# Row stores of the tail bunched behind the last attention values, and slot 1's row gathers moved behind the last store

## The chip, the cores and the metric

One NeuronCore of a Trainium2 chip runs the whole program. The metric is the device time in microseconds (us) of one execution. TensorE is called PE, VectorE DVE, ScalarE ACT, GpSimd POOL and SyncE SP; "PE issue" in the profile is time in which PE waited for nothing that the profile shows.

## The reference

Chunked attention feeds a mixture of experts with one expert per row. The attention works on 8 x 8 heads of 576 rows in chunks of 64; its output, 4608 rows of 512, is routed.

```python
scores = scale * np.matmul(q_c, k_c.transpose(0, 1, 2, 4, 3))
attn = np.exp(scores - max); attn = attn / (sum + 1e-09)
x = np.matmul(attn, v_c) ...            # (4608, 512)
logits = x @ w_gate                      # 8 experts
expert_idx = np.argmax(logits, axis=1)
gate_w = softmax(logits)[row, expert_idx]
out[mask] = gate_w * (np.maximum(x[mask] @ w1[e], 0.0) @ w2[e])   # for each expert e
```

## The kernel before

**Attention stage.** The 4608 rows are 36 tiles of 128 rows, in 18 groups of two tiles (the loop over `g`). Per group PE computes scores, transposes and values (`attn_v`, L283: 64 small matmuls into the banks U and V); DVE scales the values into a row buffer `xb` (`x_out`, L295); PE transposes the rows once more (`x_t`, L306) and makes the logits (`logits`, L318, then `sel_`, L899). Seven batches of tiles (6, 6, 6, 6, 4, 4, 4) go through `route`, a generator whose small DVE steps are dealt out between other work by `small_op` and `side_op`. It ends with a row index `di` (L401) for each row of the batch; POOL writes gate and row number into the buffer (L403); and the batch's tiles enter the list `waiting`.

**Sorting by expert.** `store(n, after)` (L417 to L428) takes the first `n` waiting tiles and has POOL scatter each one's 128 rows to the DRAM array `xd`, sorted by expert, with an indirect DMA (L424). Where `after` is given, ACT first copies one column of that tile into the unused last column of the first of these tiles (L422), so that the first store waits for it; this is how the kernel sets the pace of the stores. `gather(u)` (L548) fetches the two blocks of 128 rows of slot `u` from `xd` into `xg`, `gather_x(u)` (L552) a third block into `xg3`, each with an indirect DMA on POOL's queue (L543). The first two slots of expert 0 need not wait for all rows: slot 0 takes rows of the first 18 tiles, slot 1 of the first 32. `early(k)` computes their indices and, once those tiles are stored, issues `gather(k)` (L501). A gather reads `xd` as a whole for the scheduler, so it waits for all stores issued before it, and a store issued after it waits for the gather to have read.

**Expert stage.** A slot is 256 rows (and up to 128 more) through one expert: `make_xt` (L566 to L569) transposes the gathered rows and splits them into two parts, `gemm1` (L586, L593 with the extra rows) and `gemm2` (L662 to L664) multiply, `finish` (L671) scales and POOL scatters the output (L672). Slot 0 is cut into 32 half steps, the "halves" of the generator `fill`; `filler(n)` puts n of them on PE between the last steps of the attention, and a 33rd step finishes it.

**The tail.** Behind the loop L979 to L1061 order the rest by hand; all engines run in program order. In order: last transposes, `attn_v` of group 17, and the last logits, routing and index tables, with fillers in between; a loop `while active` that ends with the tables; then `store(NMAX)` (NMAX is 6), `gather_x(1)`, weight loads for slot 2 (`load_w`, L528, 1 MB each), the remaining halves, `make_xt(1)`, and slot 1.

Of the kernel before, what the change touches and what calls it, by code (L numbers as in the profile page):

```python
# [8 lines left out]
F32 = mybir.dt.float32  # L9
# [21 lines left out]
NMAX = max(BATCHES)  # L31
# [14 lines left out]
def attn_moe_kernel(ctx: ExitStack, tc: tile.TileContext, q, k, v, wg, w, out):  # L46
# [164 lines left out]
    def quads(i, hp):  # L211
        for c in range(2):
            for m in range(2):
                o = hp * 128 + c * 64
                yield (slice(c * 64, (c + 1) * 64), m, slice((i * 4 + hp) * 64, (i * 4 + hp + 1) * 64),
                       slice(m * 64, (m + 1) * 64), slice(o, o + 64), (m * 64, c * 64))
# [36 lines left out]
    def soft_c(ex):  # L253
        su = sm.tile([P, NH, 1], F32, name="su", bufs=2)
        nc.vector.tensor_reduce(su.rearrange("p (m h) o -> p m (h o)", m=2),
                                ex.rearrange("p h m k -> p m h k"), AX.X, ALU.add)
        return su

    def soft_e(su):
        suf = su.rearrange("p h o -> p (h o)")  # L260
        nc.scalar.activation(suf, suf, AF.Copy, bias=1e-9)
# [7 lines left out]
    def attn_t(ex):  # L269
        at = sp.tile([P, G, 4, 128], F32, name="at", bufs=1)  # L270
        for i in range(G):
            pt = bank("TQ", [P, 4, 128])
            for hp in range(4):
                nc.tensor.transpose(pt[:, hp, :], ex[:, i * 4 + hp, :, :].rearrange("p m k -> p (m k)"), ident)
            nc.scalar.copy(at[:, i, :, :], pt)
        return at

    def attn_v(g, at):
        px = [one["U"], one["V"]]
        for i in range(G):  # L280
            for hp in range(4):
                for po, m, fo, pi, fi, at_ in quads(i, hp):
                    nc.tensor.matmul(px[m][po, fo], at[pi, i, hp, po], vb[g % NB][pi, i, fi],  # L283
                                     start=True, stop=True, tile_position=at_)
        return px
# [131 lines left out]
    def store(n, after=None):  # L417

        for k, (b, i, t, di) in enumerate(waiting[:n]):
            x = xb[t // RB % XB][:, t % RB, :]  # L420
            if k == 0 and after is not None:
                nc.scalar.copy(x[:, XW - 1:XW], after)  # L422
            stored.add(t)
            nc.gpsimd.indirect_dma_start(  # L424
                out=xds[b % 2 * NMAX + i],
                out_offset=bass.IndirectOffsetOnAxis(ap=di[:, i, :], axis=0),
                in_=x, in_offset=None, bounds_check=NT - 1, oob_is_err=False)
        del waiting[:n]  # L428
# [4 lines left out]
    def advance(kind, side=False):  # L433


        for x in active:
            if x[1] == kind and x[2] == side and not (kind == "t" and r_live[0]):
                x[1] = next(x[0], "end")
                if x[1] == "end":
                    active.remove(x)  # L440
                return
# [28 lines left out]
    def early(k):  # L470


        B = EARLY[k]
        c0_ = sm.tile([P, B], F32, name=f"c{k}", bufs=1)
        st = sm.tile([P, B], F32, name=f"st{k}", bufs=1)
        ge = sm.tile([P, 2, B], F32, name=f"ge{k}", bufs=1)
        su = sm.tile([P, 2], F32, name=f"su{k}", bufs=1)
        S5 = [P, 2, B]
        n0 = ce[:, 0, 0:B]
        at_ = pid_h[:, 0:2] if k == 0 else g1[:, 0:2]  # L480
        yield "v"
        nc.vector.tensor_tensor_scan(c0_, n0, n0, 0.0, ALU.add, ALU.bypass)
        yield "v"
        nc.vector.memset(st[:, B - 1:B], BIG)
        yield "v"
        nc.vector.tensor_tensor(st[:, 0:B - 1], rows_b[:, 0:B - 1], n0[:, 0:B - 1], ALU.subtract)
        yield "v"
        nc.vector.tensor_tensor(ge, at_.unsqueeze(2).broadcast_to(S5),
                                c0_.unsqueeze(1).broadcast_to(S5), ALU.is_ge)
        yield "v"  # L490
        nc.vector.tensor_copy((msk0, msk1)[k][:, 0:2], ge[:, :, B - 1])
        yield "v"
        nc.vector.tensor_tensor(ge, ge, st.unsqueeze(1).broadcast_to(S5), ALU.mult)
        yield "v"
        nc.vector.tensor_reduce(su, ge, AX.X, ALU.add)
        yield "v"
        nc.vector.tensor_tensor((idx0, idx1)[k][:, 0:2], su, at_, ALU.add)
        yield None
        while not stored.issuperset(range(TE[k])):
            yield None  # L500
        gather(k)  # L501
        yield "v"
        if k == 0:
            nc.vector.tensor_scalar(add[0], c0_[:, B - 1:B], -1.0, float(BLK), ALU.mult, ALU.add)
        else:
            nc.vector.scalar_tensor_tensor(add[1], c0_[:, B - 1:B], -1.0, add[0], ALU.mult, ALU.subtract)
            yield "v"
            nc.vector.tensor_scalar(add[1], add[1], 2.0 * BLK, None, ALU.add)
        yield "v"
        nc.vector.tensor_scalar(add[k], add[k], 0.0, None, ALU.max)  # L510
        yield "v"
        if k == 0:
            nc.vector.tensor_scalar(g1, pid_h, add[0], float(BLK), ALU.subtract, ALU.add)
        else:

            nc.vector.tensor_tensor(add[1], add[1], add[0], ALU.add)
            yield "v"
            nc.vector.tensor_scalar(g1[:, 2:3], pid_h[:, 2:3], add[1], float(BLK),
                                    ALU.subtract, ALU.add)
# [21 lines left out]
    def rows_in(t, u, h):  # L541
        rows = TE[u] * P if u < 2 and h < 2 else NT
        nc.gpsimd.indirect_dma_start(  # L543
            out=t[:, :], out_offset=None, in_=xd[0:rows, :],
            in_offset=bass.IndirectOffsetOnAxis(ap=place(u, h), axis=0),
            bounds_check=rows - 1, oob_is_err=False)

    def gather(u):  # L548
        for h in range(2):
            rows_in(xg[u % 2][h], u, h)  # L550

    def gather_x(u):  # L552
        rows_in(xg3, u, 2)
# [65 lines left out]
    lo_, h0 = [], []  # L619
# [7 lines left out]
    def slot_0():  # L627

        py = None
        for i, step in enumerate(BLOCKS):  # L630
            f = BLOCKS[:i].count(step)
            flush()
            if step == "1":
                ph = bank("S", [P, BLK])
                gemm1_pe(0, f, ph, range(2))
                yield
                gemm1_pe(0, f, ph, range(2, 4))
                lo_.append((ph, relu_hi(ph)))
            else:
                if py is None:  # L640
                    py = [bank(x, [P, D]) for x in "UV"]
                gemm2(0, f, h0[f], 0, py)
                yield
                gemm2(0, f, h0[f], 1, py)
            yield
        for m in range(2):
            finish(0, m, py[m])

    def filler(n):
        for _ in range(n):  # L650
            next(fill, None)
            halves[0] -= 1

    fill, halves = slot_0(), [2 * len(BLOCKS)]
# [234 lines left out]
    st_e, st_l, st_x = {}, {}, {}  # L889
# [21 lines left out]
    def pauses():  # L911
        for x in list(active):
            if x[1] is None:
                x[1] = next(x[0], "end")
                if x[1] == "end":
                    active.remove(x)
# [17 lines left out]
    for g in range(NG):  # L934
# [9 lines left out]
        if ga >= 0:  # L944
            at = attn_t(st_e[ga])
            su = soft_c(st_e.pop(ga))
# [16 lines left out]
        if ga >= 0:  # L963
            px = attn_v(ga, at)
# [14 lines left out]
    g = NG - 1  # L979
# [3 lines left out]
    small_op(5)  # L983
    ex = st_e.pop(g)
    at = attn_t(ex)
    store(2, at[:, 0, 0, 0:1])
    filler(1)
    su = soft_c(ex)
    soft_e(su)
    store(1, su[:, 0, :])  # L990
    advance("a")
    st_x[g - 1] = x_t(g - 1, xb[(g - 1) * G // RB % XB])
    store(2, st_x[g - 1][:, 0, 0:1])
    pauses()
    small_op(7)
    advance("a")
    px = attn_v(g, at)
    filler(2)
    ri = soft_d(su)
    x_out(g, px, ri, xb[g * G // RB % XB])  # L1000
    logits(g - 1)
    store(1, st_l[g - 1][:, 0:1])
    filler(1)
    advance("t")
    small_op(5)
    advance("a")
    filler(1)
    st_x[g] = x_t(g, xb[g * G // RB % XB])
    store(2, st_x[g][:, 0, 0:1])
    sel_(g - 1)  # L1010
    filler(1)
    side_op(4)
    logits(g)
    store(2, st_l[g][:, 0:1])
    assert stored.issuperset(range(TE[1]))
    filler(1)
    sel_(g)
# [13 lines left out]
    while active:  # L1031
        for x in "cat":
            advance(x)
        small_op(2)
        pauses()
        side_op(3)
        if halves[0] > 5:
            filler(1)
        if halves[0] % 2 and h0:
            store(1, h0[-1][0][:, 0:1].bitcast(F32))  # L1040
    store(NMAX)
    assert len(stored) == NTILE
    gather_x(1)
    load_w(2, 0)
    load_w(2, 1)
# [10 lines left out]
    filler(2)  # L1056
    for c in range(2, 4):
        load_w(2, c)
    filler(halves[0] - 4)
    make_xt(1, banks="QK")  # L1060
    filler(5)  # L1061
    def slot(u, kd, nxt):
        par = wset(u)
        py = [bank("UV"[m], [P, D]) for m in range(2)]
# [127 lines left out]
```

## Time and profile before

| | |
|---|---|
| median of 3 runs | 636.71 us (634.97 to 638.28) |
| profiled execution | 635.64 us, of which 633.8 us span |
| PE busy | 588.0 us, 93% of the span |
| DVE, ACT, POOL busy | 409.7, 298.6, 271.1 us |
| mean granted clock of PE | 0.979 |

Times below are us from the start of the span. The granted clock has two levels, 1.00 (2.4 GHz) and 0.50 (1.2 GHz). A row of a timeline gives start, duration, engine, line, operation, output and inputs; in brackets the idle time of the engine before it and what ended it.

### The profile page before, as it was taken

What the parts mean: (1) busy time and instruction counts of PE and PEld (TensorE: products, weight loads), DVE (VectorE), ACT (ScalarE), POOL (GpSimd) and SP (SyncE); (2) the same over time, 40 slices, a digit from 0 to 9 for tenths busy, and PEclk for the clock granted to TensorE, in tenths of its full rate; (3) what the DMA queues carried; (4) which work ended last, traced back from release to release, by engine and by line L of the source; (5) the groups of instructions that cost most, each with busy time, mean ns of one, the idle gap of its engine ahead of it and who ended that gap; (6) DMA issues with size and microseconds to landing.
All of it is one profiled execution on the core that took longest, in us unless ns stands there. A gap on an engine that the chain in (4) does not pass through costs nothing. (4 is left out here: it accounts for less than half of the span.)

```text
span 633.8 us, 14583 instructions
## 1 busy us (share of the span) xinstructions
PE 588.0 (93%) x5775; PEld 515.8 (81%) x5775; DVE 409.7 (65%) x814; ACT 298.6 (47%) x561; POOL 271.1 (43%) x277
## 2 busy tenths in 40 slices
PE   7796979879989999999899999999899999999994
PEld 5575867758779989988798879999799899899893
DVE  6687789964836667666375647666546676676663
ACT  2565556642223455554255435544434455555452
POOL 2123445463434256435163226535412564464372
PEclk9999799997979999999999999999999999999998
DMA  8989799532284262156025402247520226421011
GB/s 315 394 279 346 244 336 314 193 140 96 100 314 156 78 198 82 36 170 218 5 72 194 157 6 77 69 163 263 205 68 29 67 72 228 124 73 36 2 35 35
DMA packets 31902, 94.88 MB, mean 150 GB/s; under 512 B 11488, under 2 KB 11488, under 8 KB 28192
## 3 DMA queue, kind: packets, MB, share of 16 engines
q0 software_dynamic: 20880, 60.74, 28.2%
q1 hardware_dynamic: 10896, 32.53, 14.4%
q8 instruction: 71, 1.16, 0.7%
q14 instruction: 55, 0.45, 0.2%
HBM read 122.65 MB, written 19.96 MB: 225 GB/s over the span
## 5 line engine op out<-in xcount | busy, mean ns | idle before, releaser
L75 DVE TENSOR_TENSOR wlo<-raw,whi 128x1024 fp32r<-128x1024 f32 x134 | 163.7, 1222 | 39.1 <-ACT whi L74 32.1
L528 POOL DMA_INDIRECT raw<-in_w,widx x71 | 74.2, 1045 | 195.9 <-DVE wlo L75 140.5
L74 ACT CAST whi<-raw 128x1024 fp32r<-128x1024 f32 x134 | 140.2, 1046 | 0.4 <-DMA raw<-in_w,widx 0.4
L606 ACT ACTIVATE hh<-psS 128x256 fp32r<-128x256 f32 x110 | 42.2, 384 | 174.8 <-PE psS L586 121.3
L611 DVE SCALAR_TENSOR_TENSOR hl<-psS,hh 128x256 fp32r<-128x256 f32 x110 | 46.3, 421 | 86.2 <-ACT hh L606 50.7
L586 PE MATMUL psS<-xhi,whi 128*128 128x256 f32 x344 | 98.4, 286 | 0.2 <-DVE oid L558 0.2
L586 PE MATMUL psS<-xlo,whi 128*128 128x256 f32 x344 | 98.2, 285 | 0.3 <-DVE xlo L569 0.3
L586 PE MATMUL psS<-xhi,wlo 128*128 128x256 f32 x344 | 98.1, 285 | 0.0
L543 POOL DMA_INDIRECT xg<-xd,idx x58 | 79.6, 1373 | 22.1 <-issue 14.6
L672 POOL DMA_INDIRECT out_y<-y,oid x40 | 52.5, 1312 | 42.1 <-DVE y L671 31.1
L586 PEld LDWEIGHTS psS<-xhi,whi 128*128 128x128 f32 x344 | 66.5, 193 | 4.4 <-issue 0.8
L586 PEld LDWEIGHTS psS<-xlo,whi 128*128 128x128 f32 x344 | 66.6, 194 | 3.2 <-DVE xlo L569 0.5
L586 PEld LDWEIGHTS psS<-xhi,wlo 128*128 128x128 f32 x344 | 66.6, 193 | 0.0
L662 PE MATMUL psU<-whi,hh 128*128 128x512 f32 x144 | 58.5, 406 | 0.0
L663 PE MATMUL psU<-wlo,hh 128*128 128x512 f32 x144 | 57.0, 396 | 0.0
L662 PE MATMUL psV<-whi,hh 128*128 128x512 f32 x144 | 56.7, 394 | 0.0
L663 PE MATMUL psV<-wlo,hh 128*128 128x512 f32 x144 | 56.4, 392 | 0.0
L664 PE MATMUL psU<-whi,hl 128*128 128x512 f32 x144 | 56.3, 391 | 0.0
L664 PE MATMUL psV<-whi,hl 128*128 128x512 f32 x144 | 56.2, 390 | 0.0
L82 POOL TENSOR_TENSOR wlo<-raw,whi 128x512 fp32r<-128x512 f32 x16 | 20.4, 1273 | 66.2 <-ACT whi L81 51.7
L424 POOL DMA_INDIRECT xd<-xb,di x32 | 31.8, 993 | 25.4 <-ACT xb L422 15.1
L662 PEld LDWEIGHTS psV<-whi,hh 128*128 128x128 f32 x144 | 27.0, 188 | 6.6
(232 smaller groups left out, 1211.8 us busy)
## 6 DMA issues: line engine op xcount, KB each, us to landing
vb<-in_v SPq DMA_DIRECT2D x18, 512.0 KB, 3.6
kb<-in_k SPq DMA_DIRECT2D x17, 512.0 KB, 6.8
qt<-in_q SPq DMA_DIRECT2D x17, 512.0 KB, 7.4
raw<-in_w SPq DMA_DIRECT2D x16, 256.0 KB, 5.9
raw<-in_w,widx POOLq DMA_INDIRECT x71
xg<-xd,idx POOLq DMA_INDIRECT x58
out_y<-y,oid POOLq DMA_INDIRECT x40
kb<-in_k SPq DMA_DIRECT2D x2, 256.0 KB
```

The lines of the kernel that those rows point to most:

```text
L74: nc.scalar.copy(hi, src)
L75: nc.vector.tensor_tensor(lo, src, hi.bitcast(F32), ALU.subtract)
L424: nc.gpsimd.indirect_dma_start(out=xds[b % 2 * NMAX + i], out_offset=bass.IndirectOffsetOnAxis(ap=di[:, i, :], axis=0), in_=x, in_offset=N ...
L528: nc.gpsimd.indirect_dma_start(out=raw[c][:, :], out_offset=None, in_=w, in_offset=bass.IndirectOffsetOnAxis(ap=widx[:, u, c:c + 1], axis= ...
L543: nc.gpsimd.indirect_dma_start(out=t[:, :], out_offset=None, in_=xd[0:rows, :], in_offset=bass.IndirectOffsetOnAxis(ap=place(u, h), axis=0 ...
L586: nc.tensor.matmul(ph, a, b[:, kc, 0:BLK], start=kc + i == 0, stop=kc + i == 5)
L606: nc.scalar.activation(hh, ph, AF.Relu)
L611: nc.vector.scalar_tensor_tensor(hl, ph, 0.0, hh.bitcast(F32), ALU.max, ALU.subtract)
L662: nc.tensor.matmul(py, hh, wh, start=f == 0, stop=False)
L663: nc.tensor.matmul(py, hh, wl, start=False, stop=False)
L664: nc.tensor.matmul(py, hl, wh, start=False, stop=f == 7)
L672: nc.gpsimd.indirect_dma_start(out=outs[m], out_offset=bass.IndirectOffsetOnAxis(ap=oid[u % 3][0:n, m:m + 1], axis=0), in_=y, in_offset=No ...
```

## The change

In the loop nothing changes. In the tail the paced stores are taken out; one `store` of up to six tiles stands behind `attn_v` of group 17 and waits for a column of bank U, and further stores of all that is waiting, without pacing, stand behind the last logits steps and in each round of the last loop. `early(1)` no longer issues `gather(1)`; it stands behind the last store, ahead of `gather_x(1)`. One more half of slot 0 comes ahead of `make_xt(1)`, one fewer behind it.

```diff
         while not stored.issuperset(range(TE[k])):
             yield None
-        gather(k)
+        if k == 0:
+            gather(0)
...
     at = attn_t(ex)
-    store(2, at[:, 0, 0, 0:1])
     filler(1)
     su = soft_c(ex)
     soft_e(su)
-    store(1, su[:, 0, :])
     advance("a")
     st_x[g - 1] = x_t(g - 1, xb[(g - 1) * G // RB % XB])
-    store(2, st_x[g - 1][:, 0, 0:1])
...
     px = attn_v(g, at)
+    store(NMAX, px[0][:, 0:1])
     filler(2)
     ri = soft_d(su)
     x_out(g, px, ri, xb[g * G // RB % XB])
     logits(g - 1)
-    store(1, st_l[g - 1][:, 0:1])
+    store(NMAX)
...
     st_x[g] = x_t(g, xb[g * G // RB % XB])
-    store(2, st_x[g][:, 0, 0:1])
+    store(NMAX)
...
     logits(g)
-    store(2, st_l[g][:, 0:1])
+    store(NMAX)
...
         if halves[0] > 5:
             filler(1)
-        if halves[0] % 2 and h0:
-            store(1, h0[-1][0][:, 0:1].bitcast(F32))
-    store(NMAX)
+        store(NMAX)
     assert len(stored) == NTILE
+    gather(1)
     gather_x(1)
...
-    filler(halves[0] - 4)
+    filler(halves[0] - 3)
     make_xt(1, banks="QK")
-    filler(5)
+    filler(4)
```

## Rows read from the trace of the kernel before

**Rows 1.** The page: the granted clock of PE in 40 equal slices of the span, in tenths.

```profile
PEclk9999799997979999999999999999999999999998
```

**Rows 2.** Waits of PE, from 126 us to 182 us: who waited for what, us in total, times, longest.

```profile
PE psT L575 <- DMA xg<-xd,idx: 3.6, 1, 3.6
PE psU L283 <- issue: 2.5, 4, 1.1
```

**Rows 3.** Timeline of PE, 126 us to 156 us: the values of group 16 (129.19 on) and of group 17 (136.44 on), and what follows each.

```profile
129.19 0.27 PE L283 MATMUL psU<-vb,at 64*64 64x64 f32 x1
...
130.36 0.64 PE L318 MATMUL psL<-xT,wg_sb 128*32 128x256 f32 x8
...
136.44 0.27 PE L283 MATMUL psU<-vb,at 64*64 64x64 f32 x1
...
137.17 0.25 PE L283 MATMUL psU<-vb,at 64*64 64x64 f32 x1
137.88 0.25 PE L283 MATMUL psU<-vb,at 64*64 64x64 f32 x1 [0.46 <-issue]
...
143.38 0.58 PE L586 MATMUL psS<-xhi,whi 128*128 128x256 f32 x1
```

**Rows 4.** Windows: length, then busy us (and instructions) of PE, PEld, DVE, ACT, POOL, the granted clock, the share of the DMA engines that was busy, GB/s.

```profile
128.00:131.00 3.00, 3.00 (x87) 2.31 (x86) 2.88 (x5) 1.47 (x4) 2.57 (x4) 1.00 0.48 186
137.00:143.00 6.00, 2.28 (x42) 1.46 (x32) 0.61 (x4) 1.16 (x4) 3.89 (x4) 0.94 0.56 214
153.00:159.00 6.00, 6.00 (x45) 5.39 (x43) 3.35 (x21) 1.51 (x8) 3.65 (x5) 1.00 0.46 180
...
143.38:149.17 5.79, 5.79 (x35) 4.58 (x34) 2.31 (x7) 1.18 (x4) 0.91 (x1) 0.50 0.01 3
...
176.55:183.47 6.92, 6.24 (x20) 5.84 (x21) 1.07 (x4) 1.14 (x3) 4.27 (x5) 0.51 0.93 368
```

**Rows 5.** Timeline of POOL, 130 us to 175 us: stores (L424), copies into the row buffers (L403), gathers (L543), the first weight load for slot 2 (L528).

```profile
135.84 0.99 POOL L424 DMA_INDIRECT xd<-xb,di  x1 [0.47 <-issue]
...
140.96 0.97 POOL L424 DMA_INDIRECT xd<-xb,di  x1 [0.30 <-issue]
148.26 0.97 POOL L424 DMA_INDIRECT xd<-xb,di  x1 [6.32 <-ACT xb L422]
...
156.40 0.97 POOL L424 DMA_INDIRECT xd<-xb,di  x1 [0.30 <-issue]
...
160.13 1.07 POOL L543 DMA_INDIRECT xg<-xd,idx  x1 [2.57 <-DVE kb L756]
161.51 1.01 POOL L543 DMA_INDIRECT xg<-xd,idx  x1 [0.30 <-DVE idx L727]
162.52 0.67 POOL L403 COPY xb<-ft 128x4 f32<-128x4 f32 x2
165.57 1.05 POOL L424 DMA_INDIRECT xd<-xb,di  x1 [2.38 <-ACT hh L606]
...
169.59 0.97 POOL L424 DMA_INDIRECT xd<-xb,di  x1 [0.31 <-issue]
173.15 1.05 POOL L543 DMA_INDIRECT xg<-xd,idx  x1 [2.58 <-DVE y L671]
174.50 1.01 POOL L528 DMA_INDIRECT raw<-in_w,widx  x1 [0.30 <-issue]
```

**Rows 6.** Timeline of PE, 156 us to 186 us: the transposes of slot 1 (L566), the last halves of slot 0 and the transposes of slot 1's extra rows (L575).

```profile
169.21 0.60 PE L566 MATMUL psQ<-ident,xg 128*128 128x128 f32 x4
...
170.78 0.39 PE L662 MATMUL psV<-whi,hh 128*128 128x512 f32 x1
...
171.48 0.39 PE L662 MATMUL psU<-whi,hh 128*128 128x512 f32 x1
...
172.61 0.39 PE L664 MATMUL psV<-whi,hl 128*128 128x512 f32 x1
176.55 1.11 PE L575 MATMUL psT<-ident,xg 128*128 128x128 f32 x4 [3.55 <-DMA xg<-xd,idx]
```

**Rows 7.** Timeline of ACT: the step ahead of the place where the new pacing copy stands (137.90), and the first cast of slot 2's weights (188.14) with the step behind it.

```profile
137.90 0.26 ACT L371 ACTIVATE eg<-lg 128x32 f32<-128x32 f32 x1
...
188.14 1.05 ACT L74 CAST whi<-raw 128x1024 fp32r<-128x1024 f32 x1 [0.40 <-DMA raw<-in_w,widx]
191.33 0.38 ACT L606 ACTIVATE hh<-psS 128x256 fp32r<-128x256 f32 x1 [2.13 <-PE psS L593]
```

**Rows 8.** Timeline of DVE: the row indices of batches 5 and 6.

```profile
149.58 0.18 DVE L401 TENSOR_REDUCE di<-dst 128x4 int32<-128x32 f32 x1
...
158.51 0.19 DVE L401 TENSOR_REDUCE di<-dst 128x4 int32<-128x32 f32 x1
```

**Rows 9.** Timeline of PE in the attention loop: two idle times, with the instruction that ends each.

```profile
28.03 0.49 PE L274 MATMUL psT<-ident,ex 128*128 128x128 f32 x3 [2.88 <-issue]
...
88.56 0.33 PE L274 MATMUL psQ<-ident,ex 128*128 128x128 f32 x1 [2.18 <-issue]
```

**Rows 10.** Windows of 6 us that begin where the two idle times of rows 9 end (columns as in rows 4).

```profile
28.03:34.03 6.00, 5.71 (x127) 4.42 (x130) 1.46 (x4) 4.18 (x8) 0.91 (x1) 0.72 0.64 248
...
88.56:94.56 6.00, 5.21 (x152) 4.16 (x153) 4.01 (x10) 3.81 (x9) 1.26 (x1) 1.00 0.73 269
```

**Rows 11.** Waits of PE, from 182 us to the end: the longest.

```profile
PE psT L566 <- issue: 2.7, 2, 1.6
```

## The prediction

> **What bounds the kernel now.** I read the page first, then the waits of PE by stretches, then the timelines of PE and POOL where PE waits. PE is busy for 93% of the span, so what counts is where it isn't, or where it runs at the lower clock. The page's clock line dips three times, and two of the dips lie between 142 us and 190 us, in the tail that the diff edits [rows 1]. From 182 us to the end PE's longest wait comes to 2.7 us in all [rows 11]: behind the tail PE is the bound, and a shift of slot 1's start moves the end by as much.
>
> In the tail PE loses time at two places, each followed by a stretch at the 1.2 GHz level.
>
> First, the values of group 17. The same 64 matmuls take 1.17 us for group 16 (129.19 to 130.36) and 6.94 us here (136.44 to 143.38) [rows 3]. From 137.17 on they come in small clumps, and the profile says "issue": no engine or transfer that it knows of holds them. The stretch coincides with five stores in a row on POOL, started from 135.84 to 140.96 [rows 5]. Behind it, from 143.38 to 149.17, the granted clock is 0.50 [rows 4].
>
> Second, the extra rows of slot 1. The halves of slot 0 end at 173.00 (172.61 plus 0.39), the transposes of the extra rows start at 176.55, and a gather ends that wait of 3.55 us [rows 2, 6]. The next 6.92 us run at 0.51 [rows 4]. This wait has a chain on POOL: gather(1) starts at 160.13, when the stores before it have landed; the last four stores start only at 165.57, 4.06 us after its second half was issued; gather_x(1) follows the last of them by 3.56 us (169.59 to 173.15), and its rows are used 3.40 us later [rows 5, 6]. So gather(1) stands in the way of the last stores, and through them of gather_x(1).
>
> **What could be gained.** The stall of the values is 6.94 - 1.17 = 5.8 us. The low clock behind it costs 5.79 x (1 - 0.50) = 2.9 us. Together 8.7. The wait for the extra rows is 3.55 us, the clock behind it costs 6.24 busy us x 0.49 = 3.1. If all went and nothing came in its place: 15.4 us. That is the floor of the range.
>
> **The change, step by step.** *Pacing.* Ten copies on ACT go and one comes; ACT is busy for a quarter of the time there [rows 4], so nothing is gained or lost there. The new one reads a column of bank U that the first value matmuls write; on ACT it stands behind the step that ends at 138.16 [rows 7], so the first store can start at about 138.6, whether the values are done or not. Queued behind it on POOL are five more stores and the row copies of batch 5; on ACT only slot 0's next step, which waits for PE anyway.
>
> *The stall.* Between 135.84 and 138.6 POOL now stores nothing. If the stores cause the stall, the values end at about 137.7, and all that PE does next is 8.7 us earlier. If they don't, it stays. The trace bounds this by zero and 8.7 us. I take the full gain, since the clumps begin and end with that burst to within about 1.5 us; the other end is a rival below.
>
> *The stores.* They are 1.28 us apart (135.84 to 140.96 in four steps) [rows 5]. With the stall gone: six from 138.6 to 145.0, done at 146.0; row copies of 0.7 us (the 0.67 us row, with a gap) [rows 5]; four from 147.0 to 150.8, done at 151.8; row copies; four from 152.8 to 156.65. Batch 6's indices, ready at 158.70 now [rows 8], would be ready at 150.0, in time. So the last store starts 12.9 us before today's 169.59.
>
> *The gathers.* Nothing of gather(1) lies ahead of the last stores any more. It starts 3.56 us after the last store at 160.2, its second half 1.38 us later at 161.6 (the step from 160.13 to 161.51), gather_x(1) at 163.0. From start to use I take 3.40 us (gather_x's row) to 4.06 us (from gather(1)'s second start to the store behind it) [rows 5]. So the first block is there at 163.6 to 164.3, the second at 165.0 to 165.7, the extra rows at 166.4 to 167.1. Behind gather(1) on POOL stand gather_x(1), four weight loads and slot 0's output scatters.
>
> *PE.* The moved half takes 0.70 us (170.78 to 171.48) [rows 6]. PE reaches slot 1's transposes at 169.21 + 0.70 - 8.7 = 161.2 and now waits for what it used to find ready: 2.4 to 3.1 us for the first block, then about 1 us for the second. Queued behind on PE are three halves and slot 1 itself; no other filler is left to cover it. The second transposes end 0.6 us after their rows, three halves take 2.1 us, so PE is through at 167.7 to 168.4, say 168.05. The extra rows are there by then, and that wait is gone. Against 176.55 this is 8.5 us earlier.
>
> *The clock there.* After an idle time of 2.88 us in the loop the next 6 us were granted 0.72; after one of 2.18 us, 1.00 [rows 9, 10]. The new wait of 2.4 to 3.1 us is nearer to the first, so I keep the dip: its 3.1 us are not gained. If the clock holds, the gain is 11.6 us.
>
> *Weights.* The first load for slot 2 starts at 174.50 and is cast at 188.14, after a wait of 0.40 us for it [rows 5, 7]: 13.6 us on the way. It would now start at 164.3 and land at 177.9. With slot 1 starting 8.5 us earlier the cast comes at 179.6 and waits for nothing; with the clock up as well it comes 3.1 us sooner and ACT waits some 1.4 us, which the 2.13 us that ACT idles right behind that cast [rows 7] cover. Without that cover it would cost those 1.4 us.
>
> **The sum.** Against the profiled execution of 635.64 us: 635.64 - 8.5 = 627.1. The median of the runs is 1.07 us above it, so the forecast is **628.2**; with the clock up, 625.1. The floor is 635.64 + 1.07 - 15.4 = 621.3.
>
> **Rivals.** *The stall stays.* Then PE is as late as now. For it speaks that from 128 us to 131 us stores moved as densely (0.48 of the DMA engines) beside the values of group 16, which ran at full pace, PE busy 3.00 of 3.00 us [rows 4]. Against it speaks only the coincidence in time. The stores: six from 138.6; four from 150.0, behind batch 5's indices (149.76); four from 158.95, behind batch 6's (158.70) [rows 8], to 162.8. Gathers at 166.35, 167.7 and 169.1; the second block is there at 171.1 to 171.8, PE waits from 169.9 in two pieces of no more than 1.2 us, is through at about 174.15, and the extra rows are there. Gain 176.55 - 174.15 = 2.4, and 3.1 for the clock, since no idle time is near 2.88 us: 5.5, so **631.2**; 634.3 if the clock falls.
>
> The Trainium skill (DMA: Bandwidth & Descriptors, Queues, rings and completion order) says that each DMA engine takes turns between the queues that have work, a packet at a time. By that, a transfer on another queue, PE's instructions among them, should not be held up for 6 us by a queue of stores, and the time would be this rival's, 631.2. The 128 to 131 us row agrees with it, the 137 to 143 us row doesn't show why it should fail there.
>
> *The stall moves.* If five stores in a row cost 5.8 us, ten in a row may cost 11.5 us, wherever PE then is: slot 0's halves. Everything, the last stores included, is then 5.7 us later than in the rival above: 631.2 + 5.7 = **636.9**, no change. Against it: from 153 us to 159 us, with four stores in a row, PE worked through its halves busy 6.00 of 6.00 us at 1.00 [rows 4].
>
> *The last stores are held by something else.* The profile puts the wait before 165.57 to ACT's hh [rows 5], not to the gather. If what holds them stays, they start at 165.57 as now, and gather(1) comes behind them: 173.15 and 174.5, the second block at 177.9 to 178.6, PE through at about 180.95, 4.4 us later than 176.55, with the clock low as now: **641.1**, slower. Adding up the steps from the first of the four stores (4.02 + 3.56 + 1.38 + 3.73 + 0.6 + 2.1 = 15.4 us), it gets slower as soon as that store starts later than 161.2.
>
> **Chances.** The stall goes: 0.55, of it 0.30 with the dip of the clock and 0.25 without. It stays: 0.25. It moves: 0.12. The stores stay held: 0.08. The likeliest is 628.2. The range from 621.5 (the floor) to 634.5 (the stall stays and the clock falls) leaves out the last two. A measurement of this kernel tells about 0.5% from no change, 3.2 us: faster is under 633.5. The first case and most of the second (0.22) lie there: 0.77; within it 0.15; slower 0.08.
>
> **What would show it.** The values of group 17 done in about 1.2 us, with no "issue" wait, and a clock of 1.00 behind them; the last store starting near 156.7; a PE wait for xg at L566 of 2 to 3 us in place of the one at L575. If instead the L283 clumps are there again, the second case holds; if PE shows "issue" waits at L586 or L662 beside the stores, the third; if the last four stores start at 161 or later, the fourth. The prediction is wrong in its reason if the gain comes from behind slot 1's start.

## Result, and the profile after

The changed kernel takes **640.24 us** (median of 20 runs, 636.71 to 647.46), the kernel before 636.6 us beside it (20 runs): a ratio of 1.0059, 95% interval 1.0036 to 1.0083. It is slower by 0.6%, where 628.2 us was forecast. The profiled execution took 638.60 us, with a span of 636.7. (The line numbers after the diff are one higher: L586 is now L587, L593 is L594, and so on.)

The page of the kernel after, granted clock in 40 slices. Of the two dips in the tail the first is deeper than before (the tenth slice shows 6 instead of 7), the second less deep (the twelfth shows 8 instead of 7) [rows 1].

```profile
PEclk8899889996989999999999999999999999999998
```

Waits of PE from 126 us to 190 us (who for what, us in total, times, longest). The two waits of [rows 2] are gone, the clumps of the values and the 3.6 us for the extra rows. Two others have come.

```profile
PE psL L318 <- issue: 6.2, 1, 6.2
PE psS L594 <- issue: 4.9, 1, 4.9
...
PE psK L567 <- DMA xg<-xd,idx: 0.4, 1, 0.4
```

Timeline of PE, answering to [rows 3, 6]. The values of group 17 start at 136.91, and at 138.00 the next half runs: 1.1 us instead of 6.94. Then PE stands from 144.40 (144.12 plus 0.28) to 150.61, and from 176.71 to 181.61.

```profile
136.91 0.27 PE L283 MATMUL psU<-vb,at 64*64 64x64 f32 x1
...
138.00 0.39 PE L587 MATMUL psS<-xhi,whi 128*128 128x256 f32 x1
...
142.21 0.60 PE L306 MATMUL psT<-ident,xb 128*128 128x128 f32 x4
142.64 0.60 PE L306 MATMUL psQ<-ident,xb 128*128 128x128 f32 x4
...
144.12 0.28 PE L587 MATMUL psS<-xhi,wlo 128*128 128x256 f32 x1
150.61 1.08 PE L318 MATMUL psL<-xT,wg_sb 128*32 128x256 f32 x8 [6.21 <-issue]
...
173.53 0.66 PE L567 MATMUL psK<-ident,xg 128*128 128x128 f32 x4 [0.44 <-DMA xg<-xd,idx]
...
176.11 0.60 PE L576 MATMUL psT<-ident,xg 128*128 128x128 f32 x4
181.61 1.57 PE L594 MATMUL psS<-xhi,whi 128*128 128x384 f32 x4 [4.91 <-issue]
```

Timeline of ACT: who holds PE each time. PE's L318 needs the two copies xT, which wait for PE's own transposes (L306); PE's L594 needs the cast of the extra rows, which waits for PE's transposes at L576.

```profile
148.59 0.59 ACT L308 COPY xT<-psT 128x512 f32<-128x512 f32 x1 [5.28 <-remote]
149.97 0.59 ACT L308 COPY xT<-psQ 128x512 f32<-128x512 f32 x1 [0.80 <-remote]
...
173.12 0.59 ACT L569 CAST xhi<-psQ 128x512 fp32r<-128x512 f32 x1 [2.64 <-PE psQ L567]
174.23 0.59 ACT L569 CAST xhi<-psK 128x512 fp32r<-128x512 f32 x1 [0.52 <-PE psK L567]
...
180.97 0.59 ACT L578 CAST xhi<-psT 128x512 fp32r<-128x512 f32 x1 [6.16 <-remote]
```

The transposes at L576 were issued at 176.11 and end, as modelled, at 176.71; ACT gets their completion 4.26 us later, at 180.97. Those of L306 end, as modelled, at 142.81 and 143.24, and PE goes on to its L587 matmuls until 144.40; ACT's copies start at 148.59 and 149.97, 5.8 and 6.7 us later. The releaser reads "remote" where it should read "PE". So the chain is PE, a late completion, ACT, PE. I call it a **late completion**.

Timeline of POOL, answering to [rows 5], and windows, answering to [rows 4] (same columns). Ten stores stand in one row; three gathers, four weight loads and two output scatters in another, from 168.73 to 180.5. The late completions lie in these two rows, the second of them ending 0.5 us behind its row. Not every completion in such a row is late: in the second one ACT's casts at 173.12 and 174.23 follow PE's transposes at once.

```profile
138.63 0.98 POOL L424 DMA_INDIRECT xd<-xb,di  x1 [2.78 <-ACT xb L422]
...
150.34 0.97 POOL L424 DMA_INDIRECT xd<-xb,di  x1 [0.30 <-issue]
...
159.95 0.31 POOL L403 COPY xb<-ft 128x4 f32<-128x4 f32 x2 [8.44 <-DVE dst L396]
160.87 0.98 POOL L424 DMA_INDIRECT xd<-xb,di  x1 [0.61 <-POOL xb L403]
...
164.71 0.97 POOL L424 DMA_INDIRECT xd<-xb,di  x1 [0.30 <-issue]
168.73 1.28 POOL L544 DMA_INDIRECT xg<-xd,idx  x1 [3.05 <-DMA xd<-xb,di]
...
179.47 1.00 POOL L673 DMA_INDIRECT out_y<-y,oid  x1 [0.30 <-issue]
```

```profile
143.00:151.00 8.00, 1.79 (x17) 1.39 (x19) 0.85 (x7) 1.42 (x4) 6.32 (x9) 0.79 0.54 210
151.00:158.00 7.00, 6.75 (x29) 5.02 (x22) 2.23 (x12) 1.06 (x4) 0.51 (x2) 0.51 0.14 54
...
182.00:186.00 4.00, 4.00 (x16) 4.00 (x16) 0.41 (x3) 0.39 (x2) 0.00 (x0) 0.61 1.02 324
```

### The profile page after: what moved, and what is told of

The parts are those of the page before. It is cut to its first block, busy times and chain, and to the rows that moved or that the text cites. A ratio compares the mean times of both kernels' runs of the same rounds, so it can differ in the third digit from the quotient of the medians.

```text
span 636.7 us, 14567 instructions
## 1 busy us (share of the span) xinstructions
PE 587.9 (92%) x5775; PEld 514.2 (81%) x5775; DVE 411.1 (65%) x814; ACT 297.8 (47%) x552; POOL 271.2 (43%) x277
## 4 chain that ended last, share of the span: by engine, by line
PE 45%; DMA 14%; issue 12%; DVE 3%; POOLq 3%; POOL 2%; ACT 1%; another core or an unknown queue 1%; DVEq 0%; ACTq 0%
DMA out_y<-y,oid 13%; PE psS L587 11%; PE psS L594 6%; PE psL L587 3%; PE psV L663 3%; PE psV L664 3%; PE psV L665 3%; PE psU L664 3%; PE psU L663 3%; PE psU L665 3%; POOLq L1136 2%; POOL raw L529 2%; PE psL L594 2%; PE psK L663 1%; PE psK L664 1%
## 5 line engine op out<-in xcount | busy, mean ns | idle before, releaser
L587 PE MATMUL psS<-xhi,whi 128*128 128x256 f32 x344 | 97.9, 285 | 0.2 <-DVE oid L559 0.2
L587 PE MATMUL psS<-xlo,whi 128*128 128x256 f32 x344 | 97.8, 284 | 0.3 <-DVE xlo L570 0.3
L587 PE MATMUL psS<-xhi,wlo 128*128 128x256 f32 x344 | 97.7, 284 | 0.0
L587 PEld LDWEIGHTS psS<-xhi,whi 128*128 128x128 f32 x344 | 66.2, 193 | 4.2 <-issue 0.6
L587 PEld LDWEIGHTS psS<-xlo,whi 128*128 128x128 f32 x344 | 66.2, 192 | 3.2 <-DVE xlo L570 0.5
L587 PEld LDWEIGHTS psS<-xhi,wlo 128*128 128x128 f32 x344 | 66.1, 192 | 0.0
L424 POOL DMA_INDIRECT xd<-xb,di x32 | 31.8, 992 | 18.2 <-ACT xb L422 8.9
```

The source lines that it names most:

```text
L587: nc.tensor.matmul(ph, a, b[:, kc, 0:BLK], start=kc + i == 0, stop=kc + i == 5)
```

## The experiments

The kernel before ran beside each series of experiments, on the same chip. Its median was 636.93, 636.42 and 638.69 us in three of the series, and 626.97 and 629.21 us in two. These are called the **long** and the **short** series, because the difference turned out to be part of the answer; the two traces above are of the long kind (636.6 us). The runs e9, e11, e17 and e18, which leave out the tokens' values, are single executions. Ratios are to the kernel before of the same series. Theory: a row of indirect DMAs on POOL makes PE's completions late, so the rows' place and length decide. Rivals: the stalls belong to PE's or ACT's own instructions; or to the bytes that are moved.

### The change in parts (long series, before 636.93)

**e1_stores**: the diff's stores alone; gather(1) and the halves stay where they were.

```diff
-        if k == 0:
-            gather(0)
+        gather(k)
...
-    gather(1)
     gather_x(1)
```

> The kernel before with the free stores alone: gather(1) again in early(1), four halves behind make_xt(1). Theory (two mechanisms: a row of stores starves some engine of instructions for about 6 us wherever it then is; and slot 1 cannot start until ACT has got past the branch at its head, about 6.7 us after ACT's second cast of make_xt(1)): the stall of the values goes, another one comes beside the first ten stores, make_xt(1) comes 1 to 2 us sooner than in the changed kernel, so 638 to 639 us. Rival (the changed kernel lost by gather(1) coming last): the loss goes with the gather's move undone, and with the stall of the values gone the time falls well below the kernel before, to about 630 us.

Measured: 634.56 us, ratio 0.9972 (0.9935 to 1.0010). Of PE's waits from 126 us to 190 us the 6.2 us at L318 is there again, the one at slot 1's head is not:

```profile
PE psL L318 <- issue: 6.3, 1, 6.3
...
PE psS L593 <- ACT xhi L577: 0.7, 1, 0.7
```

The time lies between the two that were expected. So the stores alone bring the first new wait, in a long series. POOL here issues gather(1) at 154.48 and 155.85, and only gather_x(1) and the loads stand at slot 1's head.

**e2_gather**: the gather's move alone, on the kernel before.

```diff
-        gather(k)
+        if k == 0:
+            gather(0)
...
+    gather(1)
     gather_x(1)
```

> The kernel before with gather(1) moved behind the last store and nothing else. Theory: the stall of the values stays (its five stores are there), the last four stores no longer wait for gather(1), but make_xt(1) waits some 2.5 us for its rows, ACT's cast and so its branch come later by that, and slot 1 starts about 1.5 to 2 us later than before: about 638.4 us. Rival (the gather's move alone gains, since gather_x(1) comes sooner, and the loss is from the free stores): 634 us or less.

Measured: 637.23 us, ratio 1.0008 (0.9976 to 1.0039). The clumps of the values are back (138.54 to 145.57), L318 has no wait, and L594 has one of 2.0 us beside 1.3 and 0.6 us for the gather. The 3.55 us of [rows 2] are gone, and these three, 3.9 us together, have come for them.

**e3_no_shift**: the change, with four halves in front of slot 1's transposes left as before.

```diff
-    filler(halves[0] - 3)
+    filler(halves[0] - 4)
...
-    filler(4)
+    filler(5)
```

> The changed kernel with four halves of slot 0 behind make_xt(1), as before the change. Theory: make_xt(1) is held by the gather's rows either way, so ACT's casts come at the same time or up to 0.5 us sooner; 639.7 to 640.2 us, no difference that can be measured. Rival (the shifted half matters): 0.7 us or more.

Measured: 639.89 us, ratio 1.0043 (1.0007 to 1.0079), with 5.5 us at L318 and 3.7 us at L594. The moved half isn't the cause.

**e4_straight**: the change, with the two arms of slot 1's inner branch swapped, so that ACT falls through where it jumped.

```diff
-            with tc.If(kd < 2) as c2:
-                form_x(EXT // 2)
+            with tc.If(kd < 2 if u > 1 else kd > 1) as c2:
+                form_x(EXT // 2 if u > 1 else EXT)
```

> The changed kernel, with the two arms of the inner branch at the head of slot 1 swapped, so that the form that this data takes (128 extra rows) is the one that follows without a jump; the other slots are unchanged. Theory (ACT's 5.45 us from its branch to its next instruction are the fetch of the jumped-to code): ACT casts the extra rows as soon as PE has transposed them, slot 1 starts about 4.3 us sooner and the low clock behind the wait is shorter, 633 to 636 us. Rival (ACT is late for another reason, such as the weight loads in flight): no change, 640 us.

Measured: 642.74 us, ratio 1.0113 (1.0059 to 1.0166), with 4.2 us at L594. The branch is out as a cause. So are blocks of instructions on their way: the DMA queues that the profile marks "instruction" have no packet from 167.84 us to 189.91 us of this trace, over the whole wait at L594, and none from 139.70 us to 161.70 us of the first trace, over the whole wait at L318.

### Where the rows stand, and what they move (long series, before 636.42)

**e5_spaced**: the tail's stores in twos, each pair held by a later step.

```diff
-    store(NMAX, px[0][:, 0:1])
+    store(2, px[0][:, 0:1])
...
-    store(NMAX)
+    store(2, st_x[g][:, 0, 0:1])
```

> The changed kernel, but its stores of the tail go in twos again, each pair held by a step of the attention, of the router or of slot 0 (the first by the first values of group 17, as in the change), and the early indices of slot 1 no longer wait for a store. gather(1) stays behind all stores. Theory (a row of stores behind one another makes PE's completions late, by up to 5.6 us, and PE idle 6.2 us at L318): with no more than two in a row the values of group 17 take 1.2 us, PE shows no idle time over 2 us between 136 and 156 us, and the time falls by 5 to 8 us against the changed kernel's 640.2, to 632 to 635. Rival (the waits at L283 and L318 belong to that stretch of PE's own instructions, whatever POOL stores): an idle time of about 6 us is there again and the time stays at 638 to 641. In both, PE's wait at slot 1's head (4.9 us at L594) stays where POOL starts the gathers and loads behind one another.

Measured: 635.12 us, ratio 0.9978 (0.9941 to 1.0014). No wait at L318, PE idle 1.02 us at most there, but the edit did less than meant: after the first pair the stores stand in one row again, 142.5 to 151.7. A completion is late in this row too, yet ACT alone waits for it:

```profile
153.96 0.38 ACT L607 ACTIVATE hh<-psS 128x256 fp32r<-128x256 f32 x1 [5.25 <-remote]
```

PE has further halves queued and goes on. So here a late completion costs PE nothing, since its next instruction doesn't need the answer. (PE then waits 4.4 us for the gather and 2.5 us at L594.)

**e8_loads_late**: the change, with the four weight loads behind slot 0's last half.

```diff
-    load_w(2, 0)
-    load_w(2, 1)
...
     filler(4)
+    for c in range(4):
+        load_w(2, c)
```

> The changed kernel with the four weight loads for slot 2 started behind slot 0's last half instead of between the gathers and slot 0's last halves, so that POOL's row at slot 1's head ends with the extra rows' gather, 3 to 4 us before the extra rows' transposes. Theory (the row of gathers and loads on POOL makes the completion of the extra rows' transposes late by 4.2 us): ACT's cast of the extra rows comes at once, PE idles under 1.5 us at L594 instead of 4.9; the weights come some 6 us later and may hold the first cast for slot 2 (0 to 5 us on ACT). Time 634 to 640. Rival (the 4.9 us wait hangs on the gathers or on the halves alone): the wait at L594 stays at 4 to 5 us, time 640 to 643.

Measured: 633.06 us, ratio 0.9972 (0.9935 to 1.0009), 7.2 us under the changed kernel's 640.24. L318's 6.2 us stays; at slot 1's head POOL's row ends with gather_x(1) at 172.8, and PE's waits and ACT's cast come in time:

```profile
PE psS L594 <- ACT xhi L578: 0.7, 1, 0.7
```

```profile
176.98 0.59 ACT L578 CAST xhi<-psT 128x512 fp32r<-128x512 f32 x1 [1.93 <-PE psT L576]
...
187.91 1.05 ACT L74 CAST whi<-raw 128x1024 fp32r<-128x1024 f32 x1 [1.24 <-DMA raw<-in_w,widx]
```

In the changed order, then, the second new wait goes with the loads behind the gathers. Loads in a row are not enough for it: in the kernel before, gather_x(1), four loads and two output scatters stand in one row from 173.15 to 182.04, and the extra rows' transposes, which end at 177.66 in the middle of it, are answered at once:

```profile
177.70 0.59 ACT L577 CAST xhi<-psT 128x512 fp32r<-128x512 f32 x1 [6.78 <-PE psT L575]
```

Starting 7 us later (180.09 instead of 172.93) costs the loads' first cast a wait of 1.24 us.

**e9_thin**: the change, with 64 bytes a row in stores and gathers (thin rows).

```diff
-    xd = dpool.tile([NT, XW], F32, name="xd")
+    xd = dpool.tile([NT, XW - D], F32, name="xd")
...
-                in_=x, in_offset=None, bounds_check=NT - 1, oob_is_err=False)
+                in_=x[:, D:XW], in_offset=None, bounds_check=NT - 1, oob_is_err=False)
```

> The changed kernel with thin rows: each row that is stored and gathered has 16 columns (gate, row number, fillers) instead of 528, 64 bytes instead of 2112. It leaves out the tokens' 512 values in stores and gathers, so the MLP works on zeros; every instruction and index stays. It tells the bytes of the stores from their issue. If the bytes that the stores move make PE's completions late: no wait over 2 us at L318 nor at L594, values in 1.2 us; 8 to 11 us less than the changed kernel, about 630. If it is POOL's issue of the stores, or the number of descriptors: PE idles 5 to 6 us at L318 as before and 4 to 5 us at L594, about 638 to 640.

Measured: 632.72 us, 6.2 us at L318 and 3.1 us at L594. The window shows what is going on meanwhile (columns as in rows 4): PE 0.77 us busy of 7, the DMA engines 3%.

```profile
142.00:149.00 7.00, 0.77 (x11) 0.26 (x9) 0.00 (x0) 1.17 (x2) 5.62 (x8) 0.85 0.03 6
```

The bytes are out, in a single execution here and again in e17. For the Trainium skill's turns between queues (DMA: Bandwidth & Descriptors, Queues, rings and completion order) this means that the trace doesn't contradict it: with idle DMA engines it has nothing to say about this wait.

**e10_later**: the change, with the ten stores held until L308's copies are done.

```diff
-    store(NMAX, px[0][:, 0:1])
...
-    store(NMAX)
+    store(NMAX, st_x[g][:, 0, 0:1])
```

> The changed kernel with its ten stores in a row held until group 17's transposes of x are copied (L318, about 5 us later than in the change); all else as in the change. Theory (the row makes PE late wherever PE is): L318's copies come at once, no 6 us idle there; a wait of 4 to 7 us shows up within 3 to 12 us of the first store instead, at the next place where PE hands work to ACT or DVE; time within 2 us of the changed kernel, 638 to 642. Rival (only the hand-over at L283 or L318 is open to it): no idle time over 2 us from 136 to 160 us, and 5 to 7 us less, 633 to 635.

Measured: 635.95 us, ratio 0.9979 (0.9941 to 1.0017). The row runs from 143.9 to 156.4, L318 has no wait, and PE's longest is this:

```profile
PE psS L587 <- DVE hl L612: 4.0, 3, 2.1
```

Neither side is right: the 6 us wait doesn't follow the row, but 4.0 us in three pieces come. (The piece of 2.1 us is of another kind, see e12.)

### Series in which the kernel before is short (626.97)

**e11_few** (thin rows, 16 partitions a store):

```diff
+            m = 16 if held[0] else P
...
-                in_=x[:, D:XW], in_offset=None, bounds_check=NT - 1, oob_is_err=False)
+                in_=x[0:m, D:XW], in_offset=None, bounds_check=NT - 1, oob_is_err=False)
```

> The thin-row kernel (16 columns a row) in which the fourteen stores of the tail carry 16 partitions each instead of 128; it leaves out the tokens' 512 values and seven eighths of the tail's rows, whose places hold a row number outside the output, written once at the start. POOL still issues the same ten stores in a row. It tells POOL's issue of a store from the rows that the store names. If the number of rows (descriptors) makes PE's completions late: the 6.2 us wait at L318 of the thin-row kernel is under 1.5 us, and the time 4 to 9 us below its 632.7. If it is the issue itself: the wait at L318 stays at 5 to 6.5 us, the time within 3 us of 632.7.

**e12_later_late** (e10's and e8's edits together) and **e13_later_early** (e1's and e10's) and **e14_spaced_late** (e5's and e8's):

> Two of the runs above together on the changed kernel: the ten stores held until group 17's transposes of x are copied, and the four weight loads put behind slot 0's last half. Theory (two separate rows of POOL's, two separate delays): neither the 6.2 us wait at L318 nor the 4.9 us at L594 is there, the gains add up: 4.3 us (640.2 to 636.0) and 7.2 us (640.2 to 633.1), about 628.8 (627 to 632), ratio about 0.988. Rival (the gains overlap, since PE then waits for slot 1's rows): the wait for the gather at L567 grows by 2 to 4 us and the time stays at 631.5 to 634.

> The change's stores alone, with gather(1) at its old place behind its own batch's stores and not behind all stores, and the ten stores held until group 17's transposes of x are copied. Theory: no 6.3 us wait at L318 as that kernel had with the stores held by the first values, none at L594 either; 634.6 less some 4 us, about 630.5 (628 to 632.5). Rival (holding the stores makes the gathers late): gather_x(1) starts later than the 168.4 us of that kernel, PE waits 2 us or more for xg, time 633 to 636.

> The kernel with its tail's stores in twos, and with the four weight loads behind slot 0's last half. Theory: the wait at L594 falls from 2.5 us to under 1.2, the 4.4 us wait for the gather stays: 635.1 less 2 to 4 us, about 632 (630 to 634). Rival (the wait at L594 there is the gathers' work): it stays at 2 to 3 us, time 634 to 636.

Measured: e11 612.66 us; e12 632.79, ratio 1.0089 (1.0061 to 1.0118); e13 634.12, ratio 1.0097 (1.0065 to 1.0129); e14 629.25, ratio 1.0037 (1.0005 to 1.0069). In none of the four traces is there a late completion: no wait at L318, 0.7 us at slot 1's head. What PE waits for is data: 3.3 us in e12 and 3.8 us in e14 for gather(1), in e13 7.64 us for the extra rows. e12 and e13 also have a 2.2 us wait for DVE's hl, as e10 had: so that one is no late completion.

The chain of e13 is the one of [rows 5], longer: gather(1) at 160.26, the stores behind it at 164.27, gather_x(1) at 171.75, PE at 175.14 (POOL's timeline, then PE's).

```profile
160.26 1.01 POOL L543 DMA_INDIRECT xg<-xd,idx  x1 [0.30 <-DVE kb L826]
...
164.27 1.05 POOL L424 DMA_INDIRECT xd<-xb,di  x1 [2.48 <-DMA xg<-xd,idx]
...
171.75 1.04 POOL L543 DMA_INDIRECT xg<-xd,idx  x1 [2.58 <-DMA xd<-xb,di]
```

```profile
175.14 1.11 PE L575 MATMUL psT<-ident,xg 128*128 128x128 f32 x4 [7.64 <-DMA xg<-xd,idx]
```

My expectations for these runs took the long series as given. e12's and e13's rivals came true, e14 ran faster than expected, and e11 can't be read alone. And why is the kernel before 10 us shorter?

### Both kernels again, long (before 638.69)

> The kernel before, unchanged, with a profile of its own. In the last series its runs had a median of 626.97 us, in the three before that 636.4 to 636.9, and no profile shows what went. If the stall of group 17's values (5.8 us, and 2.9 us of clock behind it) is what went: in a series at about 627 us the 64 value matmuls take 1.2 us and PE has no low clock at 143 us; in a series at about 636.6 us they take 7 us, as in its first trace. If it is something else (slots 1 to 17, the start): the values take 7 us in both, and the missing 9.7 us lie elsewhere.

> The changed kernel, unchanged, in the same series. In a series in which the kernel before takes 636.6 us: 640.2, PE idle 6.2 us at L318 and 4.9 us at L594. In one in which it takes 627 us: if late completions behind POOL's row come and go with the series, both waits are short (under 1.5 us) and the time is 625 to 629; if only the stall of the values comes and goes, the waits at L318 and L594 stay and the time is 638 to 641, a ratio of 1.02.

> The thin-row kernel again (rows of 16 columns, the tokens' values left out), beside the next one on one chip. In the earlier series it idled 6.23 us at L318 and took 632.7 us. The same again if the wait is of the kernel; under 1.5 us and about 620 us if it comes and goes with the series, as the kernel before does.

> The thin-row kernel with 16 partitions a store in the tail again (it leaves out the tokens' values and seven eighths of the tail's rows). It took 612.7 us with no wait at L318 in the series in which the kernel before took 627 us. If the number of rows decides: no wait over 1.5 us at L318 here, whatever the thin-row kernel shows beside it; if the series decided: the same wait at L318 in both kernels.

Measured: e15, the kernel before, 637.72 us, its values of group 17 again from 141.27 to 147.21 (5.9 us). e16, the changed kernel, 641.64, ratio 1.0043 (0.9989 to 1.0096), with 6.4 us at L318 and 5.7 us at L594. e17, thin rows, 638.17, with 7.1 and 3.7 us. e18, 16 rows a store, 638.60, where the same kernel had taken 612.66 without such waits:

```profile
PE psL L318 <- ACT xT L308: 9.7, 1, 9.7
PE psS L598 <- ACT xhi L582: 3.6, 1, 3.6
```

The number of rows is out as well: late completions come with the series.

### The changed kernel, short (before 629.21)

> The stores of the tail in twos and the four weight loads behind slot 0's last half, again. In the series in which the kernel before takes 627 us it took 629.3 (ratio 1.0037). Theory, if here the kernel before takes 636 to 639 us, with late completions: PE idles under 2 us between 136 and 156 us and under 1.5 us at L594, and it beats the kernel before by 0.6 to 1.2% (629 to 634 us). Rival: it is no more than 0.4% faster, as the run with stores in twos alone was (0.9978), since the wait for the gather (3.8 to 4.4 us) takes what the stores give.

> The changed kernel again. With the kernel before at 636 to 639 us: 640 to 642, as before, with 6.2 us of idle PE at L318 and 5 us at L594. With the kernel before at 627 us (no late completions): no such idle times; then its own order decides, and the working behind the forecast, without the 8.7 us of the stall that is gone in both, leaves PE a wait of 2 to 4 us for slot 1's first block in place of 3.55 us for the extra rows: 624 to 629, ratio 0.995 to 1.003.

Measured: e19 627.96 us, ratio 0.9976 (0.9944 to 1.0009); what it does in a long series stays untried. e20, the changed kernel, **625.65 us, ratio 0.9964 (0.9930 to 0.9999)**: faster, if by little. That little is no more than a hint, since e14 and e19 are one kernel in the two short series and stand at 1.0037 and 0.9976, further apart than e20 is from 1. ACT's timeline, then PE's, then POOL's:

```profile
141.28 0.59 ACT L308 COPY xT<-psT 128x512 f32<-128x512 f32 x1 [0.54 <-PE psT L306]
...
166.08 0.59 ACT L578 CAST xhi<-psT 128x512 fp32r<-128x512 f32 x1 [1.93 <-PE psT L576]
```

```profile
161.96 0.66 PE L567 MATMUL psQ<-ident,xg 128*128 128x128 f32 x4 [1.31 <-DMA xg<-xd,idx]
162.88 0.66 PE L567 MATMUL psK<-ident,xg 128*128 128x128 f32 x4 [0.26 <-DMA xg<-xd,idx]
165.45 0.60 PE L576 MATMUL psT<-ident,xg 128*128 128x128 f32 x4
166.72 0.98 PE L594 MATMUL psS<-xhi,whi 128*128 128x384 f32 x4 [0.68 <-ACT xhi L578]
```

```profile
137.01 0.99 POOL L424 DMA_INDIRECT xd<-xb,di  x1 [2.78 <-ACT xb L422]
...
154.63 1.00 POOL L424 DMA_INDIRECT xd<-xb,di  x1 [0.30 <-issue]
158.39 1.05 POOL L544 DMA_INDIRECT xg<-xd,idx  x1 [2.75 <-DMA xd<-xb,di]
```

The same ten stores in a row and the same loads behind the gathers as in the first trace, and the releaser of both ACT instructions is PE. The window that was nearly empty is full (143 to 151), and behind slot 1's head, where the clock was 0.61, it is 1.00 (168 to 186):

```profile
143.00:151.00 8.00, 8.00 (x60) 6.90 (x53) 5.49 (x31) 2.01 (x8) 6.06 (x12) 1.00 0.53 206
...
168.00:186.00 18.00, 18.00 (x96) 16.75 (x95) 11.81 (x36) 5.75 (x14) 5.84 (x7) 1.00 0.71 267
```

The spans of the first trace and of e20, one kernel, differ by 14.5 us (636.7 and 622.2). Of these, 13.3 lie between the first value matmul of group 17 and PE's L594 (136.91 to 181.61, 44.70 us, against 135.30 to 166.72, 31.42 us), the stretch with the two waits; from L594 to the end the two take 455.1 and 455.5 us.

No version ran clearly faster than the kernel before in both kinds of series: e8 (long) and e19 (short) are each some 0.25% below it, within their intervals.

## Why the prediction was wrong

**The step that failed is "The stall. ... I take the full gain."** The first half of it held: with no store on POOL until 138.63 the values take 1.1 us. But the time was not gained: a wait of 6.2 us came at a hand-over (work of PE that ACT takes on and gives back) inside the new row of stores (e1 shows that the stores alone bring it), and it comes in long series only. That this is the values' delay in a new place is argued from both lying beside a row of stores in long series. It isn't shown, and the two look different: in the values PE's own matmuls start in clumps though none of them waits for an answer, while at L318 PE goes on to 144.40 and its answers come late. It comes nearest to the rival "The stall moves", which had 0.12 and stood at 636.9. Its place was L318, not slot 0's halves, and its price 6.2 us and the clock behind it, 6.75 x (1 - 0.51) = 3.3, together 9.5 instead of 11.5. The argument against it, PE running at full pace beside four stores in a row [rows 4], was a weak witness: the halves there had more work queued behind, as in e5, and could have hidden a late completion.

**No case had the second wait**, at slot 1's head: 4.9 us at L594, of which 0.7 is there without late completions, and 4.00 x (1 - 0.61) = 1.6 of clock: 5.8 us in all. I had counted what is queued behind gather(1) on POOL only for when it starts, not for what its row does to others.

**The size.** The profiled execution is 638.60 - 627.1 = 11.5 us over the forecast's own sum. Against it stand 9.5 + 5.8 = 15.3 us. Two terms that the sum had in it come off: the dip of the clock that it kept there (3.1), and the wait for gather(1), 0.7 us instead of 3.4 to 4.1 (about 3), as PE comes late anyway. That leaves 9.2; 2.3 us I don't account for, 0.5 of them the later start of the values.

**The other steps held where no completion is late.** Counted from the first value matmul of group 17 (136.44 before, 135.30 in e20): first store 2.2 us forecast, 1.7 measured; last store 20.2, 19.3; first gather 23.8, 23.1; the extra rows' transposes done 31.6 (PE through at 168.05), 30.75 (165.45 plus 0.60). The wait for the first block was 1.3 us instead of 2.4 to 3.1, so the clock stayed up: 625.1 was the forecast for that case, 625.65 came out, in a series whose kernel before is itself 7.4 us shorter: so the order of the steps is borne out, the gain is not. That the stores behind gather(1) are held by it, against the rival "The last stores are held by something else", shows in e20 (the last four stores from 150.79 on, 15.5 us counted as above, forecast 16.4, with gather(1) behind them) and in e13, where the row names the gather. In the first trace they start at 160.87 because batch 6's indices are late with everything else (8.44 us of waiting for DVE's dst).

**Why that isn't 8 us of gain even in the short series.** There the kernel before takes 629.21, 7.4 us less than its first median; in the other short series 9.6 less. The stall of the values with its clock was priced at 8.7 us. That it is what went is argued from the size and from its being there in every trace of a long series; no profile of the kernel before in a short one was taken, so it isn't shown.

**Open.** What makes PE's completions late. Shown: it is not the bytes (e9, e17), not the number of rows (e18), not the branch (e4), not a block of instructions on its way (e4 and the first trace), not the moved half (e3); it comes inside or just behind rows of indirect DMAs on POOL, though not at every completion there, and where the weight loads leave such a row, the delay there leaves too (e8); it comes with the series, which these runs can't choose. The chip's number alone doesn't tell the kinds apart: the series at 636.93 and at 626.97 had the same one. Whether PE itself stands still or only its signal is late, the trace doesn't tell. The traces of the two kinds differ in one more thing: counted in them, those of long series hold 1875 to 1916 records of updates of the engines' semaphores (fourteen traces), those of short series 2055 to 2059 (six). So records are missing in long series, "remote" may stand for one of them, and whether the recording of an execution has a part in the delay was not tried.

**A slip in the range.** The floor is worked out as 621.3 and the range starts at 621.5; nothing hangs on it.

## What to carry to other kernels

A stall that coincides with a burst on another queue is not priced by its old place: ask which hand-over (PE to ACT and back to PE, with nothing queued between) lies inside the burst's new place, and count it there at full size as the bad case; in these traces it fell on some of them and spared others. Before a stall is counted as a gain, see it in traces of more than one series, since a stall that comes and goes by itself is in the time of both kernels. Independent work queued on PE covered a late completion in e5; the values of group 17, which wait for no answer either, stalled beside five stores all the same, so it is no safe cover. Loads that nobody needs soon can leave a long row of DMA issues, as in e8.

## What was not expected of the hardware

The same program differs by 7 to 12 us between series (626.97 to 638.69 for the kernel before). In long series some completions of PE reach ACT 4.3 to 6.7 us after their modelled end (first trace; 5.28 us of ACT's waiting there and again in e1), inside or just behind a row of POOL's indirect DMAs that are 1.28 to 1.3 us apart, with the DMA engines at 54% or, with thin rows, at 3%. In short series the same row delays nothing (0.54 us of ACT's waiting in e20). The traces of long series also hold 7 to 9% fewer records of updates of the engines' semaphores than those of short series.
